# One store of 128 partitions for each output tile, in place of four stores of 32 partitions for each pair of tiles

## Chip, cores and metric

One core of one Trainium2 chip. The metric is the device time of one execution in microseconds (us). The span of a profile is the time from its first to its last instruction; it is some 2 us shorter than the measured time. PE is the matmul engine (TensorE), PEld its weight loads, DVE is VectorE, ACT is ScalarE, POOL is GpSimd and SP is SyncE. The profile counts 16 DMA engines for the core; the transfers between HBM and SBUF run on them, cut into packets. A DMA share is the time that packets took, over the time of all 16 engines. The granted clock is the share of its full clock that TensorE was allowed. Lines such as L518 are lines of the kernel. Runs marked slow (over 1.5% above the fastest run of the same kernel) are left out of ratios.

## The reference

```python
# q, k, v: [8 batches, 8 heads, 576, 64]; p: [8, 8, 32, 64], all float32
def sm_attn(qq, kk, vv):                       # softmax attention
    s = scale * qq @ kk.T
    a = exp(s - max(s)); a = a / sum(a)
    return a @ vv
p_packed = sm_attn(p, k, v)                    # 32 packed tokens for each head
x = heads_joined(sm_attn(q, p_packed, p_packed))          # [8, 576, 512]
W_tok = (x @ w_q) @ (x @ w_k).T / 8
out = relu(W_tok @ x) @ w_out                  # [8, 576, 512] float32
```

A batch of the output has 576 rows of 512 float32 (2 KB). The kernel deals these rows as 32 groups (g) of 18 (r): row = 18 g + r.

## The kernel before

The program is a fixed list of steps in a hand-made order. For each of 8 batches it loads q, k and v (three loads of 576 KB as bf16, issued by POOL, which cast from float32), and computes output tiles of 128 rows. Tiles 0 to 3 of a batch hold four values of r times all 32 g each, r outermost. A fifth tile takes the last two r of two batches together (the remainder, `o_rem`); its store is not changed. The parts that matter:

```python
    inpool = ctx.enter_context(tc.tile_pool(name="inpool", bufs=NL))      # NL = 4
    opool = ctx.enter_context(tc.tile_pool(name="opool", bufs=5))
    ...
    def RL(b, j, eng, bk):
        o = new("relu", b, [P, NJ, 512], pool=epool)[:, j]
        relu(eng, o, T["mx", b, j])                 # bf16 in SBUF <- float32 in PSUM, on ACT or DVE
    ...
    def OT(b, t, *a):                               # matmuls of one output tile into PSUM
        ...
                lhsT = T["relu", b][:, j, t * P:(t + 1) * P]
    ...
    def OE(b, t, *a):                               # PSUM -> SBUF -> HBM
        ...
        tp = t // 2
        o = new("o", (b, tp), [P, 2, D], fp32, "o", opool)
        copy(eng, o[:, t % 2, x:x + w], T["ot", b, t, x])
        done[b, tp] = done.get((b, tp), 0) + w
        if done[b, tp] == 2 * D:
            dst = out[b].rearrange("(g r) n -> g (r n)", r=RQ)[:, tp * 4096:(tp + 1) * 4096]
            for s in range(4):
                queue = nc.scalar if w < D and s % 2 else nc.sync
                queue.dma_start(dst[:, s * 1024:(s + 1) * 1024],
                                o[s * GQ:(s + 1) * GQ].rearrange("a e n -> a (e n)"))
```

Rows r of an even tile and r + 1 of its odd partner lie side by side in a pair tile, so one row of a store is 4 KB. Each of the four stores reads 32 partitions.

The softmax here doesn't subtract the row's maximum and nothing guards it: scores larger than these inputs give would overflow.

Of the kernel before, what the change touches and what calls it, by code (L numbers as in the profile page):

```python
# [74 lines left out]
def kernel(  # L75
# [11 lines left out]
    nc = tc.nc  # L87
    fp32 = mybir.dt.float32
# [12 lines left out]
    D = moe_w_q.shape[0]  # L101
    Dl = moe_w_q.shape[1]
    P = 128
# [6 lines left out]
    RQ, GQ = 18, 32  # L110
# [8 lines left out]
    inpool = ctx.enter_context(tc.tile_pool(name="inpool", bufs=NL))  # L119
    bpool = ctx.enter_context(tc.tile_pool(name="bpool", bufs=NB))  # L120
    epool = ctx.enter_context(tc.tile_pool(name="epool", bufs=2))
    opool = ctx.enter_context(tc.tile_pool(name="opool", bufs=5))
    psum = ctx.enter_context(tc.tile_pool(name="psum", bufs=1, space=bass.MemoryType.PSUM))

    def bank(n, shape, dt, name):
# [2 lines left out]
    def copy(eng, o, i):  # L128
        if eng == "A":
            nc.scalar.activation(o, i, COPY)  # L130
        elif eng == "P":
            nc.gpsimd.tensor_copy(o, i)
        else:
            nc.vector.tensor_copy(o, i)  # L134
# [89 lines left out]
    T = {}  # L224

    def new(key, b, shape, dt=bf16, tag=None, pool=None):
        if (key, b) not in T:
            T[key, b] = (pool or bpool).tile(shape, dt, tag=tag or key, name=key)
        return T[key, b]
# [280 lines left out]
    def OT(b, t, *a):  # L510
        x, w = (a[0] * D // 2, D // 2) if len(a) == 3 else (0, D)
        ps = T["ot", b, t, x] = bank(a[-1], [P, w], fp32, "out_ps")
        for j in range(NJ):
# [3 lines left out]
                lhsT = T["rem", b // 2][:, j % 2 * 2 + j // 2].rearrange("a n g e -> a (n g e)")  # L517
            nc.tensor.matmul(ps, lhsT, wout[:, j, x:x + w], start=j == 0, stop=j == NJ - 1)  # L518

    def OE(b, t, *a):  # L520
        eng = a[-2]
        x, w = (a[0] * D // 2, D // 2) if len(a) == 3 else (0, D)
        if t == 4:
            o = opool.tile([P, D], fp32, tag="orem", name="o_rem", bufs=2)
            copy(eng, o, T["ot", b, t, 0])
            dst = out.rearrange("b (g r) n -> (b g) r n", r=RQ)
            queue = nc.gpsimd if b == B - 1 else nc.sync
            queue.dma_start(dst[(b - 1) * GQ:(b + 1) * GQ, RQ - 2:], o)
            return
        tp = t // 2  # L530
        o = new("o", (b, tp), [P, 2, D], fp32, "o", opool)
        copy(eng, o[:, t % 2, x:x + w], T["ot", b, t, x])
        done[b, tp] = done.get((b, tp), 0) + w
        if done[b, tp] == 2 * D:
            dst = out[b].rearrange("(g r) n -> g (r n)", r=RQ)[:, tp * 4096:(tp + 1) * 4096]
            for s in range(4):
                queue = nc.scalar if w < D and s % 2 else nc.sync
                queue.dma_start(dst[:, s * 1024:(s + 1) * 1024],
                                o[s * GQ:(s + 1) * GQ].rearrange("a e n -> a (e n)"))

    done = {}
    steps = dict(PX=PX, PXE=PXE, WC=WC, KT=KT, KE=KE, S1=S1, X1=X1, PV=PV, RC=RC, PP=PP,
                 PT=PT, PE=PE, QK=QK, QKE=QKE, QT=QT, QE=QE, S2=S2, X2=X2, RS=RS, RR=RR, AM=AM,
                 AT=AT, AE=AE, WKQ=WKQ, WE=WE, WR=WR, GM=GM, GE=GE, Y=Y, YE=YE, MX=MX, MR=MR, RL=RL, RLR=RLR,
                 OT=OT, OE=OE)

    with tc.manual_schedule():
        for item in ORDER.split():
            name, _, bk = item.partition("=")
            name, _, eng = name.partition("@")  # L550
# [41 lines left out]
```

## Time and profile before

| | before |
|---|---|
| time, median (3 runs) | 124.64 us (123.60 to 126.11) |
| span of the profile | 122.5 us |
| PE busy | 106.5 us, 87% |
| end of the last matmul | 113.0 us |
| tail from there to the end | 9.5 us |
| loads (q0), share of 16 engines' span | 68.9% |
| SP's transfers (q1), share | 25.7% |

The two transfer shares sum up to 94.6% of the span. Packets of one engine overlap (up to a share of 1.19, as the prediction reads from the trace), so over the whole run the DMA engines have some room left, but from 12 to 86 us hardly any. The lines behind this table are shown and read in the prediction below.

### The profile page before, as it was taken

What the parts mean: (1) busy time and instruction counts of PE and PEld (TensorE: products, weight loads), DVE (VectorE), ACT (ScalarE), POOL (GpSimd) and SP (SyncE); (2) the same over time, 40 slices, a digit from 0 to 9 for tenths busy, and PEclk for the clock granted to TensorE, in tenths of its full rate; (3) what the DMA queues carried; (4) which work ended last, traced back from release to release, by engine and by line L of the source; (5) the groups of instructions that cost most, each with busy time, mean ns of one, the idle gap of its engine ahead of it and who ended that gap; (6) DMA issues with size and microseconds to landing.
All of it is one profiled execution on the core that took longest, in us unless ns stands there. A gap on an engine that the chain in (4) does not pass through costs nothing.

```text
span 122.5 us, 4561 instructions
## 1 busy us (share of the span) xinstructions
PE 106.5 (87%) x1968; PEld 70.1 (57%) x1968; DVE 81.3 (66%) x197; ACT 78.2 (64%) x159; POOL 37.9 (31%) x49
## 2 busy tenths in 40 slices
PE   6989989687999999999998999989999989998000
PEld 2576746565748757568585657766585646354000
DVE  6362456667876858598864689987996988754000
ACT  3131568766779798799858888678767866464000
POOL 6949302722059004757000066600070120000200
PEclk9999999999999999999999999999999999999755
DMA  3999999999999999999999999999972526782584
GB/s 67 373 157 186 195 213 206 209 207 206 213 208 211 269 298 217 243 212 262 303 224 208 220 289 283 267 274 273 202 157 79 130 64 185 213 211 67 152 226 135
DMA packets 16485, 25.47 MB, mean 208 GB/s; under 512 B 3168, under 2 KB 11360, under 8 KB 16464
## 3 DMA queue, kind: packets, MB, share of 16 engines
q0 software_dynamic: 11872, 14.68, 68.9%
q1 hardware_dynamic: 4224, 9.64, 25.7%
q10 hardware_dynamic: 368, 0.85, 2.6%
q8 instruction: 15, 0.25, 0.7%
q14 instruction: 6, 0.05, 0.1%
HBM read 30.15 MB, written 9.44 MB: 323 GB/s over the span
## 4 chain that ended last, share of the span: by engine, by line
PE 52%; issue 16%; DVE 11%; DMA 7%; POOL 4%; ACT 3%; POOLq 1%; ACTq 0%
PE out_ps L518 14%; DMA q_sb<-in_q_dram 7%; PE qT_ps L369 6%; PE pv_ps L328 6%; PE aT_ps L423 3%; PE kT_ps L280 3%; PE e_ps L310 3%; PE e_ps L388 3%; PE mix_ps L486 2%; PE wkq_ps L444 2%; DVE kT L134 2%; DVE a L414 2%; DVE rs L404 2%; POOL wqk L169 2%; PE wkq_ps L439 2%
## 5 line engine op out<-in xcount | busy, mean ns | idle before, releaser
L414 POOL TENSOR_TENSOR a<-e,rr 128x512 bf16<-128x512 f32 (+1 forms) x12 | 15.0, 1258 | 55.2 <-DVE rr L408 34.0
L518 PE MATMUL out_ps<-wout,relu 128*128 128x512 bf16 (+1 forms) x132 | 31.4, 373 | 0.0
L518 PEld LDWEIGHTS <-relu 128*128 128x128 bf16 x132 | 11.7, 98 | 10.6 <-issue 0.4
L130 ACT ACTIVATE o<-out_ps 128x512 f32<-128x512 f32 (+1 forms) x21 | 12.3, 587 | 5.5 <-PE out_ps L518 3.8
L316 ACT ACTIVATE e<-e_ps 128x512 bf16<-128x512 f32 (+1 forms) x24 | 11.0, 490 | 7.1 <-PE e_ps L310 7.0
L404 DVE TENSOR_REDUCE rs<-e 128x16 f32<-128x512 f32 (+1 forms) x16 | 12.9, 809 | 3.2 <-ACT e L397 2.7
L397 ACT ACTIVATE e<-e_ps 128x512 f32<-128x512 f32 (+1 forms) x24 | 11.5, 524 | 4.3 <-PE e_ps L388 4.0
L134 DVE COPY o<-out_ps 128x512 f32<-128x512 f32 (+1 forms) x12 | 8.0, 664 | 5.9 <-PE out_ps L518 4.9
L496 ACT ACTIVATE relu<-mix_ps 128x512 bf16<-128x512 f32 x19 | 10.3, 600 | 1.7 <-PE mix_ps L486 1.1
L498 DVE TENSOR_SCALAR relu<-mix_ps 128x512 bf16<-128x512 f32 x13 | 8.6, 682 | 3.3 <-PE mix_ps L486 3.3
L369 PE MATMUL qT_ps<-idb,q_sb 128*64 128x128 bf16 x288 | 10.7, 220 | 0.1
L130 ACT ACTIVATE qT<-qT_ps 128x1024 bf16<-128x1024 bf16 (+1 forms) x13 | 9.3, 736 | 0.3 <-PE qT_ps L369 0.3
L559 PE MATMUL warm_ps<-warm 128*128 128x512 bf16 x26 | 8.5, 463 | 1.2 <-DVE warm L137 1.2
L369 PEld LDWEIGHTS <-q_sb 128*64 128x64 bf16 x288 | 8.7, 110 | 1.2 <-issue 0.7
L130 ACT ACTIVATE kT<-kT_ps 128x1024 bf16<-128x1024 bf16 (+2 forms) x10 | 7.3, 755 | 2.1 <-PE kT_ps L286 2.1
L388 PE MATMUL e_ps<-ppT,qT 128*128 128x64 bf16 x160 | 7.8, 193 | 0.8 <-issue 0.5
L423 PE MATMUL aT_ps<-idb,a 128*128 128x128 bf16 x80 | 7.3, 220 | 1.4 <-issue 0.7
L328 PE MATMUL pv_ps<-v_sb,e 64*64 64x192 bf16 x288 | 8.3, 246 | 0.0
L388 PEld LDWEIGHTS <-qT 128*128 128x128 bf16 x160 | 6.4, 98 | 3.0 <-issue 1.8
L134 DVE COPY qT<-qT_ps 128x1024 bf16<-128x1024 bf16 (+1 forms) x11 | 6.6, 603 | 2.1 <-PE qT_ps L369 2.1
L310 PE MATMUL e_ps<-pdiag,kT 128*64 128x64 bf16 x288 | 7.6, 197 | 0.4 <-DVE kT L134 0.2
L444 PE MATMUL wkq_ps<-aT,pqk 128*128 128x256 bf16 (+1 forms) x64 | 7.7, 233 | 0.0
(84 smaller groups left out, 192.5 us busy)
## 6 DMA issues: line engine op xcount, KB each, us to landing
out_dram<-o SPq DMA_DIRECT2D x62, 128.0 KB, 4.7
q_sb<-in_q_dram POOLq DMA_DIRECT2D x8, 576.0 KB, 15.2
v_sb<-in_v_dram POOLq DMA_DIRECT2D x8, 576.0 KB, 15.7
k_sb<-in_k_dram POOLq DMA_DIRECT2D x7, 576.0 KB, 17.1
out_dram<-o_rem SPq DMA_DIRECT2D x3, 256.0 KB, 5.9
k<-in_k_dram ACTq DMA_DIRECT2D x1, 576.0 KB, 4.3
k<-in_k_dram SPq DMA_DIRECT2D x1, 576.0 KB, 6.9
wout<-in_moe_w_out_dram POOLq DMA_DIRECT2D x2, 256.0 KB, 19.9
```

What stands on the lines that cost most here:

```text
L130: nc.scalar.activation(o, i, COPY)
L134: nc.vector.tensor_copy(o, i)
L310: nc.tensor.matmul(ps[halves(i), at[0]:at[1] + 1:at[1] - at[0]], T["kT", b][:, place(b, m), halves(i)], rhs, start=True, stop=True)
L316: nc.scalar.activation(e1[:, 2 * z0:2 * z1], T["s1", b, c], EXP, scale=scale)
L328: nc.tensor.matmul(T["pv", b][i][halves(cc)], lhsT, rhs, start=n == 0, stop=n == R - 1, skip_group_check=True)
L369: nc.tensor.transpose(ps[halves(x), z - z0], q_in[b][:, x, r * Dh:(r + 1) * Dh], idb)
L388: nc.tensor.matmul(ps[:, t - 2 * c, i, cc], lhsT, T["ppT", b][:, i, cc], start=True, stop=True)
L397: nc.scalar.activation(e2(b, min(c, 1))[:, o:o + n], T["s2", b, c].rearrange("a t i c (x l) -> a (t i c x) l", l=L), EXP, scale=scale)
L404: e.tensor_reduce(rs, T["e2", (b, d)], axis=AX, op=ADD)
L414: e.tensor_tensor(a2[:, 2 * d:2 * d + n].rearrange("a t i (u l) -> a (t i u) l", l=L), T["e2", (b, d)], T["rr", (b, d)].to_broadcast((P, n ...
L423: nc.tensor.transpose(ps[:, i, t - 2 * c], T["a2", b][:, t, i], idb)
L518: nc.tensor.matmul(ps, lhsT, wout[:, j, x:x + w], start=j == 0, stop=j == NJ - 1)
```

## The change

The intent: let each tile be stored as soon as it is copied, all 128 partitions at once, with one issue in place of two (four for each pair), and with sixteen buffers so that no copy waits for a store.

```diff
-    opool = ctx.enter_context(tc.tile_pool(name="opool", bufs=5))
+    opool = ctx.enter_context(tc.tile_pool(name="opool", bufs=16))
 ...
+    def store(o, b, r0, n):
+        d = out[b].rearrange("(g r) n -> g (r n)", r=RQ)[0:1, r0 * D:r0 * D + 1]
+        dst = bass.AP(d.tensor, d.offset, [[2 * D, 4], [RQ * D, GQ], [1, n * D]])
+        nc.sync.dma_start(dst, o)
 ...
-        tp = t // 2
-        o = new("o", (b, tp), [P, 2, D], fp32, "o", opool)
-        copy(eng, o[:, t % 2, x:x + w], T["ot", b, t, x])
-        done[b, tp] = done.get((b, tp), 0) + w
-        if done[b, tp] == 2 * D:
-            dst = out[b].rearrange("(g r) n -> g (r n)", r=RQ)[:, tp * 4096:(tp + 1) * 4096]
-            for s in range(4):
-                queue = nc.scalar if w < D and s % 2 else nc.sync
-                queue.dma_start(dst[:, s * 1024:(s + 1) * 1024],
-                                o[s * GQ:(s + 1) * GQ].rearrange("a e n -> a (e n)"))
+        o = new("o", (b, t), [P, D], fp32, "o", opool)
+        copy(eng, o[:, x:x + w], T["ot", b, t, x])
+        done[b, t] = done.get((b, t), 0) + w
+        if done[b, t] == D:
+            store(o, b, t // 2 * 8 + t % 2, 1)
```

The destination pattern reads: 4 steps of two rows, 32 steps of 18 rows, then 512 contiguous elements. Its outermost dimension has size 4.

## The prediction

k is the number of DMA engines that a store runs on. That it would be 4 for the new destination, and always the same four engines, was the assumption. The trace of the kernel before could not show it: each of the 68 transfers on q1 has 16 completion packets there (1088 packets of 4 bytes), and so has each of the 31 on q0 (496). The list of loads, stores and the rest is the packet time of each of those four engines. It sums up to 190 to 201 us, from which come 168 to 177 us of measured time; the estimate with 26 GB/s for an engine comes to 166, and 167 was settled on. Of the 2 us for the last landing the trace shows this: the last SP store was issued by 119.8 us, and the span ended at 122.5. The 2.56 us for a store in the second rival is an estimate as well; the 81 us of stores make 2.53 for each of 32. The 119 to 123 us of the first rival count a tail of about 4 us in place of 9.

> **What bounds the kernel now.** I read the page from the top: parts 1 and 2 for the busy engine, part 3 and the table of stretches for the transfers, the waits for input and output buffers, and last the end of the run.
>
> ```profile
> PE 106.5 (87%) x1968; PEld 70.1 (57%) x1968; DVE 81.3 (66%) x197; ACT 78.2 (64%) x159; POOL 37.9 (31%) x49
> ...
> PE   6989989687999999999998999989999989998000
> ...
> DMA  3999999999999999999999999999972526782584
> ...
> q0 software_dynamic: 11872, 14.68, 68.9%
> q1 hardware_dynamic: 4224, 9.64, 25.7%
> ```
>
> PE is 90% busy or more in nearly every slice up to 113 us, then does nothing for three slices. PE bounds the middle of the run. But the transfers are close behind: q0 (the loads, issued by POOL, that cast float32 to bf16) and q1 (issued by SP, nearly all stores) together fill 94.6% of the span of all 16 DMA engines. In us per DMA engine: loads 0.689 x 122.5 = 84.4, SP's transfers 0.257 x 122.5 = 31.5. The table of stretches has the detail (columns: stretch, its us, busy us and instructions of five engines, granted clock, DMA share, GB/s):
>
> ```profile
> 12.00:37.00 25.00, 22.01 (x546) 15.15 (x545) 16.93 (x46) 17.24 (x35) 7.99 (x11) 1.00 1.19 207
> 37.00:86.00 49.00, 47.44 (x1022) 33.03 (x1022) 37.96 (x92) 40.14 (x84) 16.57 (x18) 1.00 1.15 253
> ...
> 104.00:113.50 9.50, 9.04 (x54) 4.12 (x50) 5.50 (x10) 4.62 (x9) 0.00 (x0) 1.00 0.62 166
> 113.50:122.50 9.00, 0.00 (x0) 0.00 (x0) 0.00 (x0) 0.00 (x0) 0.67 (x1) 0.59 0.64 175
> ```
>
> Three things are to be seen. First, from 12 to 37 us only loads run, and the DMA share is 1.19: packets of one DMA engine overlap, so an engine that never rests gets through about 1.19 us of packet time in 1 us. I use 1.19 as its capacity. Second, from 37 to 86 us the share is 1.15: with the stores added, the DMA engines have hardly any room. Third, PE ends at 113.5, and 9 us of stores follow, at 175 GB/s: the end is set by the last stores.
>
> The loads come just in time. The weight loads of PE waited for an input twice, briefly, and a copy waited for an output buffer twice (us in all, times, longest):
>
> ```profile
> PEld L280 <- DMA k_sb<-in_k_dram: 0.5, 1, 0.5
> ...
> PEld L369 <- DMA q_sb<-in_q_dram: 0.2, 1, 0.2
> ...
> ACT o L130 <- DMA out_dram<-o: 1.5, 2, 1.2
> ```
>
> So output buffers cost 1.5 us now, and the loads have no slack to give away. The stores to compare with, from part 6 (KB each, median us from issue to landing):
>
> ```profile
> out_dram<-o SPq DMA_DIRECT2D x62, 128.0 KB, 4.7
> ```
>
> [...] q1 has 4224 packets, of which 62 x 32 (rows of 4 KB), 3 x 128, 2 x 256 and 256 are data, 3136 in all. The other 1088 are 16 for each of the 68 transfers (62 + 3 + 1 + 2). [...]
>
> **The change part by part.** It replaces 64 stores of 128 KB (32 partitions, 4 KB rows) by 32 stores of 256 KB (128 partitions, 2 KB rows). The bytes stay 8.39 MB.
>
> *Removed:* 32 issues at 0.42 us (the median on SP): 13 us of SP, which mostly waits. This is worth nothing on the path. Also removed: the wait of the even tile for its odd partner before either is stored[...].
>
> *Added:* sixteen buffers of 2 KB in place of five of 4 KB per partition, 32 KB against 20 KB, so stores may lag by four batches. It can remove at most the 1.5 us.
>
> *Changed by the pattern:* the destination is now [4][32][512 elements], since a tile's partitions are four row groups of 32. Its slowest dimension is 4; that of the source is 128. [...] Before, the destination was [32][1024], k = 16. I take this as what decides the case.
>
> [...]
> - Loads: unchanged, 84.4 us, since every load is spread over all 16.
> - Stores: each store gives each of the four engines 32 rows, so 32 x 32 = 1024 rows of 2 KB. The only 2 KB rows of before are those of the remainder stores, with a median of 96 ns in the packet records: 98 us. From q1 as a whole: 31.5 x 8.39/9.64 x 4 = 110 us[...]. I take 98 to 110.
> - The rest, over 16 engines: remainder stores, p and the first k of q1, 31.5 x 1.25/9.64 = 4; q10 0.026 x 122.5 = 3. Together 7 us.
>
> Sum 190 to 201 us; divided by 1.19, 160 to 169 us. The first transfers start some 1 us into the run and the loads fill the engines from 5 us on: add 4. At the end add 2 us for the last landing, and 2 us by which the measured time (124.64) exceeds the span (122.5). Result: 168 to 177 us. [...] an estimate with 26 GB/s for an engine (207 GB/s written by casting loads means 414 GB/s read, over 16 engines) gives for the stores 2.10 MB / 26 GB/s = 81 us, for the loads 84.4/1.19 = 71 us, for the rest 6, with the 8 us of ends 166. I settle on 167.
>
> Does the order of things spoil the sum? Up to 37 us nothing changes, as there are no stores; about 42% of the load bytes have moved by then (the GB/s row up to there, without the first transfers of SP and ACT), so 41 us of loads are left, and 81 us of stores and a few us of remainders: 37 + 41 + 81 + 3 + 4 is again 166. For idle time on the four engines, both loads and stores would have to be missing at once. Loads are prefetched two to three batches ahead and computing will now starve for them, so they are always queued; the last loads land near 110 to 135, and the last batches' ten or so tiles are 26 us of stores, about the 22 us that computing needs from the last load on. The engines stay busy to the end either way, whoever is served first.
>
> **The rivals.**
> - *The store is spread over 16 engines after all* (the pattern could be rewritten before it reaches the hardware). For it: all transfers of before have k = 16. Against it: none of them has a slowest dimension under 16. Then 1024 x 4 rows over 16 engines are 25 us each, as now[...]. Time 119 to 123 us.
> - *Four engines, but the loads don't suffer* (the stores only take what is left). Then the stores alone count: from 37 us 32 x 2.56 us = 82 us, thus 119 to 122, with a tail after the last tiles of some 8 to 10 us, time 125 to 135. Against it: every load must land on all 16 engines, four of which have no time left, and 1.15 of 1.19 is taken already.
> - *The output buffers become the bound*, with stores lagging by over sixteen tiles and copies, then PE, waiting for "out_dram<-o". It would show in the waits, but the sum of the four engines' work stays the same, so the time does, too.
>
> **Range and chances.** I give k = 4 some 93%. Within it the uncertainty is the speed of one engine: at 29 GB/s (no more shown than the best tenth of packets, 84 ns for 2 KB, times 1.19) about 150 us; without any overlap of store packets about 188. The range of 8 in 10 is 148 to 188. Faster and same take the first rival's 4% and what is left.
>
> **What would show it.** In part 3 of the new page q1 has 4096 + 1152 = 5248 data packets; with k = 4 there are 32 x 4 + 6 x 16 = 224 completions, total 5472; with k = 16 there are 38 x 16 = 608, total 5856. With k = 4 the mean DMA share of the middle falls from 1.15 to about 0.7, the average of four full engines and twelve that wait (the packet time of all 16, (84.4 + 7) x 16 + 98 x 4 = 1854 us, over 16 x 167); a store takes over 5 us to land, later tens of us; PE's weight loads wait for k_sb and q_sb by tens of us in sum; POOL's loads, 15 to 17 us to landing now, take about twice that; the tail after the last matmul grows to 10 us and more. I am wrong if q1 has 5856 packets, or if the loads' landing times stay as they are while stores are slow.

## The result, and the profile after

The changed kernel took 168.69 us (median of 4 runs, 168.55 to 168.84), against 124.14 us (123.60 to 126.11, 4 runs) for the kernel before. The ratio is 1.361, with a 95% interval of 1.353 to 1.369. A ratio here is the mean time of one kernel's fast runs over the mean of the other's fast runs of the same rounds, so it is not quite the ratio of the medians.

The page of the changed kernel: the busy tenths of PE and of the DMA engines in 40 slices of 4.18 us, what they moved, and the two main queues.

```profile
PE   7999858899799599956999766399999300000000
...
DMA  5999999999999999722596822232222332222221
GB/s 159 264 199 206 207 208 208 209 212 218 224 228 246 227 229 221 145 72 69 95 227 120 164 72 70 81 148 103 105 101 102 150 149 102 103 102 102 102 102 43
...
q0 software_dynamic: 11872, 14.68, 50.7%
q1 hardware_dynamic: 5472, 9.90, 16.3%
```

q1 has 5472 packets: 5248 of data and 224 completions (the packets of 4 bytes in its records), which is 32 stores with 4 and 6 other transfers with 16. Before, every transfer on q1 had 16. And where only stores run (152 to 164 us, below), the share of the 16 engines is 0.26, that of four. So each store runs on four engines. The DMA row shows what that looks like: from slice 18 on it often has a 2 or 3, about a quarter of the capacity, with 69 to 72 or with 102 GB/s. That is what four full and twelve idle engines give. In the slices with 69 to 81 GB/s (18, 19 and 24 to 26, counted from 1) PE falls to 3 to 6 tenths: as I read it, the twelve engines have finished their shares of the loads, and PE waits until the four have moved theirs between the stores.

The table of stretches (stretch, its us, busy us and instructions of PE, PEld, DVE, ACT and POOL, granted clock, DMA share, GB/s):

```profile
12.00:37.00 25.00, 21.00 (x536) 14.91 (x540) 16.59 (x45) 17.14 (x35) 7.26 (x9) 1.00 1.19 208
37.00:86.00 49.00, 41.78 (x806) 29.30 (x810) 29.84 (x73) 32.80 (x67) 14.43 (x16) 0.90 0.92 182
86.00:104.00 18.00, 13.57 (x300) 9.25 (x300) 13.42 (x31) 10.42 (x23) 4.71 (x4) 1.00 0.58 119
104.00:130.00 26.00, 22.97 (x267) 13.37 (x267) 16.02 (x35) 14.57 (x32) 1.05 (x1) 0.93 0.29 106
...
152.00:164.00 12.00, 0.00 (x0) 0.00 (x0) 0.00 (x0) 0.00 (x0) 0.00 (x0) 0.50 0.26 102
```

Up to 37 us the transfers are as before (1.19; 208 against 207 GB/s), as hardly a store has been issued. From 37 to 86 us PE is busy for 41.8 us, against 47.4 before. In the last stretch only stores run: 102 GB/s, or 25.5 GB/s for each of four engines.

The waits of PE and its weight loads for data (us in all, times, longest), which were 0.7 us for k_sb and q_sb together before (a wait of PE and one of its weight loads can be the same stretch of time, so their sum counts it twice):

```profile
PE pv_ps L328 <- DMA v_sb<-in_v_dram: 6.2, 4, 2.8
...
PEld L328 <- DMA v_sb<-in_v_dram: 5.2, 3, 3.0
...
PEld L369 <- DMA q_sb<-in_q_dram: 3.9, 4, 1.8
...
PEld L286 <- DMA k_sb<-in_k_dram: 2.1, 1, 2.1
...
PE kT_ps L286 <- DMA k_sb<-in_k_dram: 2.0, 1, 2.0
PEld L280 <- DMA k_sb<-in_k_dram: 2.0, 1, 2.0
```

And the chain that ended last, in order of time (start, us, what), of which these two pieces are the longest:

```profile
52.02 25.06 DMA q_sb<-in_q_dram
...
89.06 19.60 DMA v_sb<-in_v_dram
```

The added time is thus in two places. The last matmul ends at 130.8 us in place of 113.0 (17.8 us later; most of it is waiting, directly or through other engines, for late loads, and 4.4 us of it is PE's own busy time, which grew from 106.5 to 110.9 us while its granted clock was 0.90 from 37 to 86 us in place of 1.00), and the tail of stores after it takes 36.3 us in place of 9.5 (26.8 us more). The two sum up to the 44.6 us by which the span grew. SP shows the lack of engine time too: one issue of a store took 2.41 us in the median in place of 0.42, about the 2.57 us that 256 KB (262,144 bytes) take at 102 GB/s.

### The profile page after: what moved, and what is told of

Read it like the earlier page. It is cut to its first block, busy times and chain, and to the rows that moved or that the text cites. A ratio compares the mean times of both kernels' runs of the same rounds, so it can differ in the third digit from the quotient of the medians.

```text
span 167.1 us, 4508 instructions
## 1 busy us (share of the span) xinstructions
PE 110.9 (66%) x1952; PEld 74.0 (44%) x1968; DVE 82.1 (49%) x197; ACT 78.5 (47%) x159; POOL 37.9 (23%) x49
## 2 busy tenths in 40 slices
DMA packets 17636, 25.46 MB, mean 152 GB/s; under 512 B 2272, under 2 KB 10464, under 8 KB 17616
## 3 DMA queue, kind: packets, MB, share of 16 engines
q0 software_dynamic: 11872, 14.68, 50.7%
q1 hardware_dynamic: 5472, 9.90, 16.3%
## 4 chain that ended last, share of the span: by engine, by line
PE 27%; DMA 27%; issue 12%; DVE 7%; POOL 3%; ACT 2%; POOLq 0%
DMA q_sb<-in_q_dram 15%; DMA v_sb<-in_v_dram 12%; PE out_ps L518 5%; PE warm_ps L560 4%; PE qT_ps L369 4%; PE pv_ps L328 3%; PE kT_ps L286 2%; POOL a L414 2%; DVE kT L134 2%; DVE rs L404 1%; PE e_ps L310 1%; PE kT_ps L280 1%; PE px_ps L253 1%; PE aT_ps L423 1%; PE mix_ps L486 1%
## 5 line engine op out<-in xcount | busy, mean ns | idle before, releaser
L518 PE MATMUL out_ps<-wout,relu 128*128 128x512 bf16 (+1 forms) x122 | 30.6, 377 | 0.7 <-issue 0.2
L369 PE MATMUL qT_ps<-idb,q_sb 128*64 128x128 bf16 x288 | 11.8, 233 | 3.1 <-DMA q_sb<-in_q_dram 1.5
L328 PE MATMUL pv_ps<-v_sb,e 64*64 64x192 bf16 x288 | 9.2, 269 | 6.2 <-DMA v_sb<-in_v_dram 6.2
L369 PEld LDWEIGHTS <-q_sb 128*64 128x64 bf16 x288 | 9.5, 118 | 4.7 <-DMA q_sb<-in_q_dram 3.9
L328 PEld LDWEIGHTS <-e 64*64 64x64 bf16 x288 | 6.8, 117 | 8.8 <-DMA v_sb<-in_v_dram 5.2
L134 DVE COPY kT<-kT_ps 128x1024 bf16<-128x1024 bf16 (+1 forms) x13 | 7.1, 556 | 2.1 <-PE kT_ps L286 1.0
```

The lines of the kernel that those rows point to most:

```text
L134: nc.vector.tensor_copy(o, i)
L328: nc.tensor.matmul(T["pv", b][i][halves(cc)], lhsT, rhs, start=n == 0, stop=n == R - 1, skip_group_check=True)
L369: nc.tensor.transpose(ps[halves(x), z - z0], q_in[b][:, x, r * Dh:(r + 1) * Dh], idb)
L518: nc.tensor.matmul(ps, lhsT, wout[:, j, x:x + w], start=j == 0, stop=j == NJ - 1)
```

## The experiments

Theory: each of the 32 stores runs on the same four DMA engines, whose work (their part of the loads and all of the stores) sets the time. The rivals: the 2 KB rows or the size of a store cost by themselves; the lag that sixteen buffers allow piles work up at the end; only the starved loads cost. All kernels gave correct results. In this section "before" is the kernel before in the same rounds: 125.32 us in the first series, 124.02 in the second, 124.21 in the third, 125.22 in the last.

**1. The same rows and buffers, in four stores of 32 partitions.**

```diff
-        nc.sync.dma_start(dst, o)
+        for s in range(4):
+            nc.sync.dma_start(dst[s], o[s * GQ:(s + 1) * GQ])
```

> The changed kernel, but each tile goes out in four stores of 32 partitions (destination [32][512], slowest dimension 32), still in 2 KB rows, from sixteen tile buffers. Theory (four of the 16 DMA engines carry all stores): 16 engines again, so q1 has 5248 data packets and 134 x 16 = 2144 completions, 7392 in all, and the time comes back to that of before, 121 to 129 us. Rival (2 KB rows, or storing tile by tile with a long lag, is what costs): the rows, their number and the buffers are those of the change, so it stays at 160 us or more.

Measured: 129.35 us (128.02 to 129.74), ratio 1.033 (1.018 to 1.047), just above the range that was expected.

```profile
q1 hardware_dynamic: 7392, 9.90, 26.9%
```

The packet count has 16 completions for each of 134 transfers, as before the change, and 39 of the 45 us are gone, although rows, tiles and buffers are those of the change. It is 3% slower than before, by an interval that reaches below 2%. The last matmul ends at 115.9 us, the tail takes 11.9. What those 3% are made of was not taken apart: 128 issues in place of 64, rows of half the size read from 32 partitions, and the granted clock (0.943 to 0.974 against 0.960 to 0.977) all changed together.

**2. One store per tile on 16 engines, by another order of partitions.** If a tile's partitions lie as (g, r) and not as (r, g), the destination is [32][4][512]. Here the order is made where a matmul reads its moving operand.

```diff
-                nc.tensor.matmul(ps[:, e:e + c1 - c0], pqk[:, i, Dl:], aT[:, i, c0:c1],
+                rhs = aT[:, i, c0:c1]
+                if c < 2:
+                    rhs = rhs.rearrange("a (t r g) -> a t g r", t=2, g=GQ)
+                nc.tensor.matmul(ps[:, e:e + c1 - c0], pqk[:, i, Dl:], rhs,
 ...
-        dst = bass.AP(d.tensor, d.offset, [[2 * D, 4], [RQ * D, GQ], [1, n * D]])
+        dst = bass.AP(d.tensor, d.offset, [[RQ * D, GQ], [2 * D, 4], [1, n * D]])
```

> One store for each tile as in the change, same rows, same buffers, but the columns of a matmul operand are read in another order, so that the tile's partitions lie as 32 groups of 4 and the destination is [32][4][512], slowest dimension 32. Theory: 16 engines, q1 5248 + 38 x 16 = 5856 packets, reads from all partitions at once, a tail of about 4 us after the last matmul, 118 to 125 us. Rival (one store for a whole tile of 256 KB is what costs): 160 us or more. A miss of both would be a slow matmul, whose operand is now read with a stride: then the matmuls of line 444 take well over 233 ns.

Measured: 128.51 us (126.30 to 130.23). Three of its four runs, the profiled one too, count as slow, being over 1.5% above the fastest, so there is no ratio; the fast run took 126.30 against 124.03 to 125.32 for the fast runs of before. It has the 5856 packets named for 16 engines, 16 completions for each of 38 transfers. One store for a whole tile is not what costs. The gain at the end was eaten by the matmul with the strided operand, as its time shows. Groups of instructions by form (count, busy us, mean ns), first the kernel before, then this one:

```profile
L444 PE MATMUL wkq_ps<-aT,pqk 128*128 128x256 bf16 x32 | 6.0, 273 | 0.0
```

```profile
L447 PE MATMUL wkq_ps<-aT,pqk 128*128 128x256 bf16 x32 | 16.3, 600 | 0.0
```

The 32 matmuls took 10 us longer; the profiled run's last matmul ended at 122.8 us, 10 us later than before, and its tail took 5.7 us, not 9.5.

**3. Four engines with 4 KB rows and the buffers of before.**

```diff
-            for s in range(4):
-                queue = nc.scalar if w < D and s % 2 else nc.sync
-                queue.dma_start(dst[:, s * 1024:(s + 1) * 1024],
-                                o[s * GQ:(s + 1) * GQ].rearrange("a e n -> a (e n)"))
+            d = dst[0:1, 0:1]
+            dst = bass.AP(d.tensor, d.offset, [[2 * D, 4], [RQ * D, GQ], [1, 2 * D]])
+            nc.sync.dma_start(dst, o.rearrange("a e n -> a (e n)"))
```

> The kernel before, with its pairs of tiles, 4 KB rows and five buffers, but the four stores of a pair made one, with the destination [4][32][1024] and so a slowest dimension of 4. Theory: four engines, bytes as in the change, so 158 to 175 us, with waits for output buffers (five pairs hold ten tiles). q1 then has 16 x 128 + 1152 data packets and 16 x 4 + 96 completions, 3360 in all. Rival (the 2 KB rows cost): back near 124 us.

Measured: 173.59 us (172.93 to 174.24), ratio 1.390 (1.368 to 1.413).

```profile
q1 hardware_dynamic: 3360, 9.90, 15.6%
```

This is the counter-test of run 1: the kernel before, with nothing changed but that the four stores of a pair are one with an outermost dimension of 4, is as slow as the changed kernel. (That one store for a pair is not what costs is shown by runs 9 and 12, where it has an outermost dimension of 32: 128.84 and 122.70 us.) So the row size is not the cause. It is 5 us slower than the change, as I read it because the four engines ran dry once: one slice of its GB/s row, at about 127 us, has 4 GB/s.

**4. Two engines.**

```diff
-        nc.sync.dma_start(dst, o)
+        for s in range(2):
+            nc.sync.dma_start(dst[2 * s:2 * s + 2], o[s * 64:(s + 1) * 64])
```

> The changed kernel, but each tile in two stores of 64 partitions, destination [2][32][512], slowest dimension 2. Theory[...]: two engines carry all stores, both halves the same two; packet time per engine 84.4 loads + 2 x 90 stores + 7 rest = 271 us, over 1.19, and 8 us for the ends: 228 to 255 us. Completions 64 x 2 + 96 = 224. Rival (the two halves land on different engines, so four in all): near 168 us. Rival (number or size of stores counts, not the engines): 124 to 170 us.

Measured: 250.43 us (250.01 to 250.85), ratio 2.006. From its table of stretches and its page:

```profile
q1 hardware_dynamic: 5472, 9.90, 10.7%
```

```profile
200.00:240.00 40.00, 0.00 (x0) 0.00 (x0) 0.00 (x0) 0.00 (x0) 0.00 (x0) 0.50 0.13 51
```

Two halves of a tile, each on two engines, do not run beside each other on four: 51 GB/s is two engines at 25.5 GB/s, and the share of 0.13 is two of sixteen. All stores land on the same two engines.

A queue that carries one store at a time, on engines that change from store to store, would show the same 51 GB/s. The stretch from 98 to 106 us, when the last loads were still under way (their last packets ended at 108.2 us in the change and at 108.8 us here), refutes this. First the change, then this run:

```profile
98.00:106.00 8.00, 5.82 (x142) 4.20 (x142) 5.56 (x14) 3.41 (x8) 2.48 (x2) 1.00 0.29 71
```

```profile
98.00:106.00 8.00, 5.39 (x138) 4.03 (x138) 5.55 (x12) 3.78 (x8) 2.48 (x2) 1.00 0.15 37
```

Loads and stores together had a share of 0.29 and 0.15. Four of 16 engines at the capacity of 1.19 would show 0.30, two 0.15. By the packet records it was 0.16 loads and 0.11 stores in the change, and 0.08 and 0.06 here. So what was left of the loads shared four engines with the stores, here two, while the others did nothing: the stores ran on the same engines all along.

Reckoned as in the prediction, 4.19 MB at 26 GB/s for each of two engines are 161 us, and with loads, rest and ends 246. From four engines to two the time grew by 82 us, which is once more the 82 us that 2.10 MB take at 25.5 GB/s.

**5. Five buffers in place of sixteen.**

```diff
-    opool = ctx.enter_context(tc.tile_pool(name="opool", bufs=16))
+    opool = ctx.enter_context(tc.tile_pool(name="opool", bufs=5))
```

> The changed kernel with five tile buffers in place of sixteen. Theory: the four engines' work is the same and they stay busy, so 165 to 180 us, now with waits of copies for output buffers of 10 us or more in sum, where the change had none, and a shorter tail after the last matmul than its 36 us. Rival (stores that lag sixteen tiles behind and pile up at the end are what costs, so less lag is better): 150 us or less. Rival (buffers are the bound): well over 180 us.

Measured: 168.63 us, against 168.69 for the change.

```profile
ACT o L130 <- DMA out_dram<-o: 21.3, 6, 7.4
DVE o L134 <- DMA out_dram<-o: 20.3, 5, 9.0
PEld L286 <- DMA k_sb<-in_k_dram: 2.5, 1, 2.5
PE kT_ps L286 <- DMA k_sb<-in_k_dram: 2.4, 1, 2.4
```

The copies now wait 41.6 us for buffers, the waits for loads shrink from some 24 us to 5, the last matmul ends at 150.7 us and the tail takes 16.4. The time is the same. A reader of this profile alone would call the buffers the bound, and would be wrong: the eleven buffers that the change has more only move the wait.

**6. The stores held back until the loads are done.**

```diff
+    held, flag = [], const.tile([1, 16], bf16, name='flag')
 ...
-        nc.sync.dma_start(dst, o)
+        if held is None:
+            nc.sync.dma_start(dst, o)
+        else:
+            held.append((dst, o))
 ...
                 load(f[1])
+                if f[1] == "v7":
+                    nc.sync.dma_start(flag, v_bufs[7 % NL][0:1, 0:16])
+                    for dst, o in held:
+                        nc.sync.dma_start(dst, o)
+                    held = None
```

> The changed kernel, but all stores of the first sixteen tiles are held back until the last load has landed (a small transfer that reads the last load's tile goes ahead of them on the same queue). Theory: the loads then run alone on all engines, land by about 86 us as before, PE waits for no load up to then; but the four engines have 32 stores of 2.56 us = 82 us left from there: 86 + 82 + 4 = 172 us, 166 to 180. This tells apart who loses (loads or stores) from the sum: the waits must go from the loads to the output buffers and the tail, and the time must hardly move. Rival (what costs is the loads' starvation by the stores alone): with undisturbed loads the time falls to 150 us or less.

Measured: 179.02 us (178.99 to 179.05), ratio 1.441.

```profile
71.00:86.00 15.00, 14.38 (x288) 10.02 (x289) 13.23 (x32) 11.59 (x26) 6.16 (x6) 1.00 0.76 137
86.00:104.00 18.00, 9.07 (x187) 6.13 (x186) 6.93 (x19) 5.17 (x12) 2.52 (x2) 0.81 0.22 74
```

(v7 is the last load.) The loads are undisturbed: PE is busy for 14.4 of the 15 us from 71 to 86 us, and the list of waits has no wait of PE for q, k or v. The first of the stores held back goes out at 87.9 us. It doesn't help, it costs 10 us. As I read it, the reason is that the engines had time free before (share 0.76 from 71 to 86 us, against a capacity of 1.19) which the stores didn't use. So starved loads are not the cause by themselves either. They are one of two forms that the same lack of engine time takes; the tail is the other.

**7. The stores issued by POOL.**

```diff
-        nc.sync.dma_start(dst, o)
+        nc.gpsimd.dma_start(dst, o)
```

> The changed kernel with its stores issued by POOL in place of SP, pattern unchanged (slowest dimension 4). [...] Theory (always the same four engines are the bound): [...] the time falls far below 168 us; POOL pays about 0.7 us for each of 32 more issues and, as it works in order, each waits for its copy, so loads are issued later: 125 to 150 us. Rival (a store on only four engines is slow by itself, whichever they are): 160 us or more.

Measured: 132.47 us in the one fast run, 138.78 in a slow one. (On which engines POOL's stores would run was an assumption that no run shows.) The same pattern, from another issuer, costs a fifth of what it cost from SP (8.3 of 44.6 us). The trace doesn't name the engine of a packet, and POOL cut the data into 4 KB packets with many small records beside them (8800 packets under 512 B, against 2272 in the change), so on which engines each store ran, and on how many, stays open. So the run shows that the pattern is not slow from every issuer, but not why. POOL's busy time went from 37.9 to 60.6 us; what the 8 us above the kernel before are made of was not taken apart.

**8 and 9. One store on 16 engines, the order made by the relu.** Run 8 has single tiles and sixteen buffers, run 9 pairs of tiles with 4 KB rows and five buffers. Both have the outermost dimension of 32 besides (run 8 the pattern of run 2, run 9 that of run 12); the cut shows the relu alone.

```diff
-        relu(eng, o, T["mx", b, j])
+        relu(eng, o.rearrange("a (t g r) -> a t r g", t=4, g=GQ),
+             T["mx", b, j].rearrange("a (t r g) -> a t r g", t=4, g=GQ))
```

> One store per tile on 16 engines once more, but the order 32 groups of 4 is now made where the relu tile is written (a strided write), so that no matmul operand is read with a stride. Theory: without the 158 ns per matmul that the strided operand cost, PE ends at 113 to 116 us, the tail is 4 to 7 us, and the time 119 to 124 us, that is 1 to 4% below the kernel before. Miss: if the strided write is slow (relu over 700 ns in place of 600 to 680) it is 124 to 128.

> The kernel before with its pairs, 4 KB rows and five buffers, the relu tile written as 32 groups of 4, and one store for each pair, destination [32][4][1024], 16 engines, all 128 partitions. q1: 16 x 128 + 1152 + (16 + 6) x 16 = 3552 packets. Theory: fewer packets[...], but the last store waits for the whole last pair: 119 to 125 us, within 2% of the run with single tiles. If 2 KB rows do cost by themselves, this one is 2 us or more ahead of the run with single tiles.

Measured: 128.89 us, ratio 1.034 (1.027 to 1.040), and 128.84 us, ratio 1.038 (1.033 to 1.042). The named miss came about, and both times lie above every range that was named for them: relu on ACT and DVE took twice its time. (The 158 ns in the first of these expectations compares medians over two forms; the matmul concerned grew by 327 ns, as run 2 shows.) Row sizes of 2 and 4 KB gave the same time on the same chip. The relu of run 8 (minimum, median and maximum ns):

```profile
L496 ACT ACTIVATE relu<-mix_ps x19: 1307/1395/1452, 33.2 to 115.7; 128x512 bf16<-128x512 f32 x19
L498 DVE TENSOR_SCALAR relu<-mix_ps x13: 1266/1299/1349, 32.4 to 116.0; 128x512 bf16<-128x512 f32 x13
```

**10. The same, with the loops of the relu the other way round.** The tile in SBUF has the same contents as in run 8, but it is written contiguously and the source in PSUM is read with a stride of 32 float32. The store is that of run 8.

```diff
-        relu(eng, o, T["mx", b, j])
+        relu(eng, o.rearrange("a (t g r) -> a t g r", t=4, g=GQ),
+             T["mx", b, j].rearrange("a (t r g) -> a t g r", t=4, g=GQ))
```

> As the run with the relu tile written in groups of 4 and single-tile stores on 16 engines, but with the same strided access put on both sides of the instruction being equal in meaning: only the way the pattern is written in the source differs. A repeat in effect: 127 to 130 us, relu 1.2 to 1.4 us each; it shows how far two builds of the same thing differ.

That expectation is a mistake: I had the two dimensions' order down as a mere way of writing, but it decides which side is walked with a stride. Measured: 120.82 us (120.14 to 122.12), ratio 0.971 (0.963 to 0.978), faster than both kernels.

```profile
q1 hardware_dynamic: 5856, 9.90, 23.7%
```

```profile
L496 ACT ACTIVATE relu<-mix_ps x19: 592/597/624, 31.8 to 107.5; 128x512 bf16<-128x512 f32 x19
L498 DVE TENSOR_SCALAR relu<-mix_ps x13: 653/680/692, 30.9 to 107.8; 128x512 bf16<-128x512 f32 x13
```

The relu costs what it cost before (600 and 682 ns). The last matmul ends at 113.4 us, as before, and the tail takes 5.7 us in place of 9.5. The first 3 us of that tail, and the first 6.3 of the tail of the kernel before, in the table of stretches:

```profile
113.50:116.50 3.00, 0.00 (x0) 0.00 (x0) 0.21 (x1) 0.34 (x1) 0.67 (x1) 1.00 0.83 313
```

```profile
113.50:119.80 6.30, 0.00 (x0) 0.00 (x0) 0.00 (x0) 0.00 (x0) 0.67 (x1) 0.62 0.75 198
```

313 against 198 GB/s at a similar share. So the form that the change intended, one store for each tile, does gain 3% once it runs on 16 engines. Against the changed kernel this is the nearest test of all: same tiles, rows and buffers, one store for each tile, 48 us less.

**11. The kernel before, with its four stores in another order.** Does the tail of before get faster when stores next to each other in the queue read from different halves of the partitions?

```diff
-            for s in range(4):
-                queue = nc.scalar if w < D and s % 2 else nc.sync
+            for s in (0, 2, 1, 3):
+                queue = nc.scalar if w < D and s > 1 else nc.sync
```

> The kernel before with one thing changed: the four stores of a pair go out in the order of partitions 0, 64, 32, 96 in place of 0, 32, 64, 96 (and in the last pair SP takes 0 and 32, ACT 64 and 96), so that neighbours in the queue read from different halves of the partitions. [...] the tail shrinks from 9 to about 7 us and the time by 1 to 2%: ratio 0.98 to 0.99. If not: 1.00 within 0.5%.

Measured: 124.19 us, ratio 1.000 (0.993 to 1.007). No effect. The condition that is cut from the expectation was a guess at why the tail of the kernel before moves 198 GB/s in its first 6.3 us, against 267 GB/s in 3.6 us of run 8's tail, where stores read 128 partitions; no run shows the reason.

**12. Run 10's relu with the pairs, 4 KB rows and five buffers of before.**

```diff
-        relu(eng, o, T["mx", b, j])
+        relu(eng, o.rearrange("a (t g r) -> a t g r", t=4, g=GQ),
+             T["mx", b, j].rearrange("a (t r g) -> a t g r", t=4, g=GQ))
 ...
-            for s in range(4):
-                queue = nc.scalar if w < D and s % 2 else nc.sync
-                queue.dma_start(dst[:, s * 1024:(s + 1) * 1024],
-                                o[s * GQ:(s + 1) * GQ].rearrange("a e n -> a (e n)"))
+            d = dst[0:1, 0:1]
+            dst = bass.AP(d.tensor, d.offset, [[RQ * D, GQ], [2 * D, 4], [1, 2 * D]])
+            nc.sync.dma_start(dst, o.rearrange("a e n -> a (e n)"))
```

> The kernel before with its pairs, 4 KB rows and five buffers; relu written contiguously while its PSUM source is read in the order 32 groups of 4, and one store per pair, destination [32][4][1024], 16 engines. It joins the relu order of the last series (ratio 0.971 with single tiles and 2 KB rows) with the row size of the kernel before. If whole 128-partition stores on 16 engines are what gained there, 119 to 122 us, ratio 0.96 to 0.985, relu 600 to 680 ns each, a tail after the last matmul of 4 to 6 us against 9. If the sixteen single tile buffers were what gained, 123 us or more.

Measured: 122.70 us (121.06 to 124.54), ratio 0.981 (0.970 to 0.992), with a tail of 6.3 us, just over the range that was expected. Three of its six runs count as slow; the fast ones took 121.06 to 122.36. The interval lies below 1 but reaches above 0.98, so a gain of 2% is not certain; whole 128-partition stores seem to gain without the sixteen buffers too. Beside run 3 it shows the dimension alone once more: one store of 4 KB rows for each pair, five buffers, and 51 us less. Run 10 and this one ran on different chips, and their intervals overlap; whether single tiles are better than pairs stays open.

## Why the prediction was right

The range was 148 to 188 us with 167 as its middle; 168.69 was measured.

- **k = 4, always the same four engines.** Right. The packet count named for it, 5472, is the one measured; run 3 puts the loss into the kernel before, run 1 takes 39 of 45 us back, run 10 takes back all of it with the two outer dimensions exchanged (and the relu's order changed to fit), and run 4 shows with two engines that they are always the same. Which four of the 16 they are no trace shows, as it doesn't name the engine of a packet. That there would be four was assumed, and no trace of the kernel before could have shown it.
- **The four engines' work is a sum, whoever is served first.** Right within limits. Five buffers (run 5) left it at 168.63 us with wholly different waits; holding stores back (run 6) cost 10 us, and the pairs of run 3 cost 5 us, both, as I read them, because engine time went unused. The argument holds as long as there is always something queued.
- **The terms.** Loads: predicted 84.4 us per engine in packet time, measured 0.507 x 167.1 = 84.7. Stores: predicted 98 to 110 us, measured 90.5 (the 2 KB packets took 88 ns in the mean over all 4480 of them, by the packet records). The capacity of 1.19 was read where only loads run; where only stores run (152 to 164 us) the share of 0.26 is 1.04 for each of four engines, so there the packets hardly overlap. The stores' packets were shorter than I took them to be and overlapped less, and these two misses nearly cancel, which is luck. The rate comes out at 25.5 GB/s for an engine. I had 26, taken from casting loads and not from stores, so that 167 fell so near 168.69 is in part luck, too; the packet sum alone gave 168 to 177. That the other twelve engines had less to do made little difference: the 2 KB packets took 88 ns in the mean on four engines and 91 in run 10 on 16.
- **Signs in the new profile.** The tail of 36.3 us is within "10 us and more", but says little. The waits for loads are a miss in size: I named tens of us of PE's weight loads for k_sb and q_sb, and they were 8.0; only with v_sb, the largest with 11.4, and with PE's own waits beside them does the sum come to some 24. The mean share of about 0.7 is right over the whole span (50.7, 16.3 and some 2% for the rest make 69%), not for "the middle", where it was 0.92 from 37 to 86 us. The loads' landing times are a miss: I said about twice 15 to 17 us, and the medians are 19 to 21, as I read it because over 40% of the loads' bytes have moved before stores are queued; the slowest of q went from 22.6 to 30.7. The last loads landed at 108 us, just before the 110 to 135 of the prediction. The page gives no landing times for the new stores, so that sign stays unchecked.
- **Slips in the working, without weight.** PE has a 9 in 27 of the 37 slices up to 113 us, which is less than "nearly every". The first k was waited for as well (0.7 us), so the weight loads waited three times, not twice. Two of the 64 stores ran on q10, so q1 carried 8.13 MB of these stores, and the rest of q1 is 1.51 MB or 5 us, not 4.
- **The rivals.** 16 engines after all: refuted for the change by the packet count. Its 119 to 123 us were close to what run 10 then measured for such a store (120.82 us, with a tail of 5.7 us). "The loads don't suffer": refuted by their waits, and by the last loads, whose last packets ended at 108 us in place of 91. "Output buffers become the bound": in run 5 they look like it, and the time is the same, as the prediction argued.

## What to carry to other kernels

Before a store is reshaped, look at the outermost dimension of its destination. In these runs a store from SP with 4 outermost ran on four of the 16 DMA engines (4 completions for each store, 102 GB/s when only stores ran), one with 2 on two, always the same ones (2 completions, 51 GB/s), and one with 32 on all 16 (16 completions; 313 GB/s in the first 3 us of run 10's tail). Loads, with 16 completions each, were held up by the stores on four engines: the waits of PE and its weight loads for k, q and v went from 0.7 to some 24 us, added up. In a profile, look for a DMA share that sits at a round fraction (0.26 for four of 16) with a low rate (102 GB/s), and count completion packets; the waits for buffers or loads only show where the lack comes to light. Where an order of rows has to be changed to get the dimension right, try it where it costs nothing: here a contiguous write of the relu, with float32 read from PSUM 128 bytes apart, was free (597 ns on ACT and 680 on DVE, against 597 and 682 in the kernel before), while a bf16 write with a stride of 4 elements (1395 and 1299 ns) and a matmul with 256 columns of bf16 read 64 bytes apart (600 ns in place of 273) about doubled the time of their instructions.
